# Sparse attention with a gated product behind it: scores over 232 keys instead of 256

## The chip, the cores and the metric

The kernel runs on one core of a Trainium2 chip. The metric is the device time of one execution in microseconds (us); the time of a version is the median over its runs. A core has the engines TensorE (PE; its weight loads are shown apart as PEld), VectorE (DVE), ScalarE (ACT), GpSimd (POOL) and SyncE (SP, which issues the DMA transfers here). Each works through its own queue of instructions in order.

## The reference

Inputs are q, k and v of 4 batches, 8 heads, 768 positions and 64 columns in float32, the numbers n_global = 8 and n_local = 96, and three weight matrices that reach the kernel as 64-bit floats. For each batch and head:

```
scores = q @ k.T / 8
rel = query position - key position
keep = (key < n_global) | ((rel >= 0) & (rel < n_local))
dist = n_local where only the first condition keeps the key, else |rel|
scores = scores - 2**-(head + 1) * dist, -1e9 where not kept
a = softmax(scores) (the sum gets 1e-9 added)
x = a @ v, put together as (3072, 512)
```

The result is `(x @ w_a * (x @ w_b)) @ w_out`, with w_a and w_b of 512 x 1536 and w_out of 1536 x 512. A query at position p needs the first 8 keys and the 96 keys that end with p. For a block of 128 queries that makes 8 first keys, up to 95 keys ahead of the block and its own 128.

## The kernel before

The 3072 positions are 24 blocks of 128 queries, six to a batch. They are put into eight units of 4, 2, 3, 3, 3, 3, 3 and 3 blocks. For each unit the attention is computed and then the product (here called the projection stage). The attention of unit u + 1 is computed during the projection stage of unit u, so that all engines share both kinds of work; only unit 0's attention stands alone at the start, beside the loading of the weights.

**Keys of a block (class Plan, L61 to L107).** Each block but the first of a batch is given a window of 256 keys: G = 32 first keys, the LW = 96 ahead and its own 128. Block 0 has its 128 own keys alone. Block 1's window of 256 is block 0's window and its own keys behind it (`joined`), so their keys are stored once. `kkeys` is the list of the unit's key columns, `kwin` the start and width of each block's window in it, `vkeys` and `vslot` the value chunks of 128 rows. The host packs q, k and v in this order (`pack`), and a DMA brings the keys and queries of a head (`fetch`, tile raw) or the values of two heads (`fetch_v`, tile v).

**Scores.** Units 2 to 7 (L784 to L801): `split` makes of the queries a rounded part qh and a rest ql, and of the keys a tile kk whose 128 partitions hold the rounded part and the rest (L351 is the subtraction, L341 and L343 are the copies); two float32r matmuls per block and head (L793) accumulate `ps[:, :w]`. Units 0 and 1 (`quad`, L668 to L679): full float32 matmuls (L673) straight from raw, for two blocks and the two heads of a pair, each with 64 partitions. A full float32 matmul leaves two records in the trace.

**Softmax (L530 to L600).** For each window: one VectorE operation adds the bias from the tile rel (`negd`; col or `negd0` for block 0) and finds the row's extreme (L537); ScalarE takes the exponential with its sum (L553); two small VectorE operations make the reciprocal (L568, L575); the normalisation is done by ScalarE (L585) or VectorE (L587). Each costs by the window's width w.

**Transposes and values.** `turn` (L602) transposes the window in chunks of 128 columns on TensorE (L609) and copies them out of PSUM; `values` (L614) multiplies each chunk with its value chunk (L626).

**Projection stage (L815 to L927).** For each of 12 columns blocks f of the weights: matmuls L851 with 128 times the unit's blocks columns (512, 256 or 384), their product on VectorE (L890), the split of it, and matmuls L869 of 512 columns. The weights are loaded and turned into a float32r part and a rest during unit 0's projection stage (`load_w`, L359 to L435), for each f in two halves of 768 columns: ScalarE L381 and L418, VectorE L388, L398, L408, L427, a copy L341 or L343 and a subtraction L351.

**Order.** `Schedule.order` (L193) is a list scheduler on the host. Every operation has a due time and estimated costs on the engines that may do it (functions act, dve, pool and pe), and the order and the choice of engine follow from these. The costs of scores, softmax and key splits are functions of w and hk.

**Start.** `build_positions` and `build_masks` make rel and col: VectorE and GpSimd operations over 256 and 128 columns, once.

Of the kernel before, what the change touches and what calls it, by code (L numbers as in the profile page):

```python
# [12 lines left out]
F32 = mybir.dt.float32  # L13
# [5 lines left out]
ALU = mybir.AluOpType  # L19
# [3 lines left out]
B, H, S, D = 4, 8, 768, 64  # L23
DM, DFF = 512, 1536
P = 128
# [2 lines left out]
NF = DFF // P  # L28
WN = 3 * 512 // 2
NT = B * S  # L30
G = 32
LW = 96

PAIRED = 2
# [14 lines left out]
BIG = float(2**38)  # L49
# [11 lines left out]
class Plan:  # L61
# [4 lines left out]
    def __init__(self, blocks, paired):  # L66
        self.nb = len(blocks)
        self.kkeys = []
        self.vkeys = []
        self.kwin = []  # L70
        self.vslot = []
        self.parts = []
        for n, (b, blk) in enumerate(blocks):
            if blk == 0:
                keys = np.arange(P)
            else:
                q0 = blk * P
                keys = np.concatenate([np.arange(G), np.arange(q0 - LW, q0 + P)])
            joined = blk == 1 and n > 0
            if paired and n % 2 == 0:  # L80
                self.parts.append(len(self.kkeys))
            if joined:
                self.kwin.append((self.kwin[-1][0], 2 * P))
                self.kkeys += [(b, j) for j in keys[P:]]
                self.vslot.append([self.vslot[-1][0], len(self.vkeys)])
                self.vkeys.append((b, keys[P:]))
            else:
                self.kwin.append((len(self.kkeys), len(keys)))
                self.kkeys += [(b, j) for j in keys]
                slots = []  # L90
                for c in range(len(keys) // P):
                    slots.append(len(self.vkeys))
                    self.vkeys.append((b, keys[c * P : (c + 1) * P]))
                self.vslot.append(slots)
        self.nk = len(self.kkeys)
        self.nv = len(self.vkeys)
        self.k0 = self.nb * P
        self.ncol = self.k0 + self.nk // 2
        if paired:

            ends = self.parts[1:] + [self.nk]
            self.pieces = []
            at = 0
            for k, end in zip(self.parts, ends):
                self.pieces.append((at, at + 2 * P - k, 2 * P + end - k, (k, end)))
                at += 2 * P + end - k
            self.ncol = at  # L107
# [198 lines left out]
class Fast:  # L306
# [223 lines left out]
    def softmax(self, h, due, wins, ps, t, sm):  # L530

        nc, op, n = self.nc, self.plan.op, len(wins)
        for j, (o, w) in enumerate(wins):
            neg = self.negd if w == 2 * P else self.negd0
            op(
                due,
                lambda e, j=j, o=o, w=w, neg=neg: nc.vector.tensor_tensor_reduce(  # L537
                    t[:, o : o + w],
                    ps[:, o : o + w],
                    neg[:, :w],  # L540
                    -(2.0 ** -(h + 1)),
                    3.0e38,
                    ALU.add,
                    ALU.min,
                    sm[:, j : j + 1],
                ),
                [ps, neg],
                [(t, j), (sm, j)],
                dve=dve(w) + 10,
            )  # L550
            op(
                due,
                lambda e, j=j, o=o, w=w: nc.scalar.activation(  # L553
                    t[:, o : o + w],
                    t[:, o : o + w],
                    AF.Exp,
                    bias=sm[:, j : j + 1],
                    scale=-1.0,
                    accum_out=sm[:, n + j : n + j + 1],
                ),  # L560
                [(sm, j)],
                [(t, j), (sm, n + j)],
                act=act(w) + 200,
            )
        sums = [(sm, n + j) for j in range(n)]
        op(
            due,
            lambda e: nc.vector.tensor_scalar_add(sm[:, 2 * n : 3 * n], sm[:, n : 2 * n], 1e-9),  # L568
            sums,
            [(sm, "e")],  # L570
            dve=69,
        )
        op(
            due,
            lambda e: nc.vector.reciprocal(sm[:, 3 * n : 4 * n], sm[:, 2 * n : 3 * n]),  # L575
            [(sm, "e")],
            [(sm, "r")],
            dve=75,
        )
        for j, (o, w) in enumerate(wins):  # L580

            def norm(e, j=j, o=o, w=w):
                r = sm[:, 3 * n + j : 3 * n + j + 1]
                if e == "act":
                    nc.scalar.mul(t[:, o : o + w], t[:, o : o + w], r)  # L585
                else:
                    self.engine(e).tensor_scalar(  # L587
                        t[:, o : o + w], t[:, o : o + w], r, 1.0, op0=ALU.mult, op1=ALU.mult
                    )

            op(
                due,
                norm,
                [(sm, "r")],
                [(t, j)],
                port=BOTH,
                dve=130 + 0.52 * w,
                pool=243 + 0.836 * w,
                act=act(w) + 100,
            )  # L600

    def turn(self, due, wins, t, pt, pf):  # L602

        nc = self.nc
        w = sum(w for o, w in wins)

        def emit(e):
            for c in range(0, w, P):
                nc.tensor.transpose(pt[:, c : c + P], t[:, c : c + P], self.ident)  # L609

        self.plan.op(due, emit, [t], [pt], pe=w / P * 109)
        self.copy(due, lambda: pf[:, :w], lambda: pt[:, :w], w, [pt], [pf], psum=True)

    def values(self, due, pl, blocks, v, probs, pa):  # L614

# [22 lines left out]
    def quad(self, u, c, j, due, raw, v, pa, homes):  # L638


        nc, pl, op, sp = self.nc, PLANS[u], self.plan.op, self.sbuf
        at, k0, _, _ = pl.pieces[j]
        blocks = (2 * j, 2 * j + 1)
        n = f"{u}_{c}_{j}"
        wins, o = [], 0
# [5 lines left out]
        qs, q0 = (raw, at) if scaled else (sp([P, cols], F32, tag, "qs" + n, 2), 0)  # L651
# [31 lines left out]
        for s in range(2):  # L683
            turn = 2 * (len(pl.pieces) * c + j) + s
            pick = lambda k: homes[k][turn % len(homes[k])]
            tag, cols = pick("t")
            t = sp([P, cols], F32, tag, f"t{s}_{n}", 2)
            sm = sp([P, 8], F32, "sm", f"sm{s}_{n}", 6)
            self.softmax(2 * c + s, due, wins, ps[s], t, sm)
            pt = self.bank(pick("pt"), f"pt{s}_{n}")  # L690
            pf = t
            if homes["pf"]:
                tag, cols = pick("pf")
                pf = sp([P, cols], F32, tag, f"pf{s}_{n}", 2)
            self.turn(due, wins, t, pt, pf)
            for i, (o, w) in zip(blocks, wins):
                probs[s, i] = (pf, o)
        if pa is None:
            pa = self.bank("psS", f"pa{n}")
        self.values(due, pl, blocks, v, probs, pa)  # L700
# [467 lines left out]
def build_positions(nc, cp, tp):  # L1168


    rel = cp.tile([P, 2 * P], F32, name="rel")
    col = cp.tile([P, P], F32, name="col")
    for t, step, base, mult in ((rel, -1, P, 1), (col, 1, 0, 0)):
        nc.gpsimd.iota(
            t,
            [[step, t.shape[1]]],
            base=base,
            channel_multiplier=mult,
            allow_small_or_imprecise_dtypes=True,
        )  # L1180
    t = tp.tile([P, 2 * P], F32, name="after")
    nc.vector.tensor_scalar(t, rel, 0.0, BIG, op0=ALU.is_lt, op1=ALU.mult)
    nc.vector.tensor_tensor(rel, rel, t, op=ALU.max)
    return rel, col, t


def build_masks(nc, rel, col, t, nf):

    v, ng, nl = nc.vector, nf[:, 0:1], nf[:, 1:2]
    v.tensor_scalar(t, rel, nl, -BIG, op0=ALU.is_ge, op1=ALU.mult)
    v.tensor_scalar(col, col, ng, -BIG, op0=ALU.is_ge, op1=ALU.mult)
    v.tensor_sub(rel, t, rel)
    v.tensor_scalar(col, col, nl, None, op0=ALU.subtract)
    v.tensor_copy(rel[:, :G], col[:, :G])
    v.tensor_tensor(col, rel[:, P:], col, op=ALU.max)


def build_scales(nc, cp):  # L1200
# [21 lines left out]
def build(nc, a, out):  # L1222
    with tile.TileContext(nc) as tc, ExitStack() as ctx:
        cp = ctx.enter_context(tc.tile_pool(name="c", bufs=1))
        with tc.manual_schedule(), tc.tile_pool(name="tmp", bufs=1) as tp:
# [2 lines left out]
            lim = build_limits(nc, cp)  # L1228
            spare = cp.tile([P, 1], F32, name="spare")
            nc.scalar.activation(spare, lim[:, 0:1], AF.Exp)  # L1230
            rel, col, t = build_positions(nc, cp, tp)
            sc = build_scales(nc, cp)
            raw0 = build_first(nc, cp, a["qkv"], sc)
            ident = cp.tile([P, P], F32, name="ident")
            make_identity(nc, ident)
            nf = build_counts(nc, cp, nv)
            flag = build_flag(nc, cp, nf, lim)
            build_masks(nc, rel, col, t, nf)
        fast = nc.values_load(flag[0:1, 0:1], min_val=0, max_val=2**30)
        inner = ctx.enter_context(ExitStack())  # L1240
        main = Fast(inner, tc, a["qkv"], a["wts"], out, raw0, (rel, col, sc, ident))
# [10 lines left out]
def pack(q, k, v):  # L1252
# [6 lines left out]
    for u, (blocks, pl) in enumerate(zip(UNITS, PLANS)):  # L1259
# [19 lines left out]
                        cols.append(np.vstack(a))  # L1279
                put(QOFFS[u][c], np.hstack(cols))  # L1280
        for c in range(NCC):
            vs = [v[b, 2 * c + s, keys] for s in range(2) for b, keys in pl.vkeys]
            put(VOFFS[u][c], np.hstack(vs))
    return flat

# [30 lines left out]
```

## Time and profile before

| what | value |
| --- | --- |
| time, median of 3 runs | 778.75 us (777.14 to 778.99) |
| profiled execution: time | 777.36 us |
| profiled execution: span of the trace | 775.1 us |
| TensorE, weight loads, VectorE, ScalarE, GpSimd busy | 751.5, 663.6, 438.7, 433.7, 6.6 us |
| mean granted TensorE clock | 0.995 of full |
| DMA | 58.04 MB, 75 GB/s in the mean |

The span is the time from the first to the last instruction on the core; 2.26 us of the profiled execution's time lie outside it. An engine's busy time is the union of its instructions' times. Matmuls overlap in their pipeline, so the duration of one is longer than the time for which it holds the queue.

### The profile page before, as it was taken

The numbers are of one execution on the slowest core, as the hardware profiler recorded it, in microseconds if no ns is written. First come the engines' busy times: TensorE is split into PE (matmuls) and PEld (weight loads), VectorE is DVE, ScalarE is ACT, GpSimd is POOL, SyncE is SP. The second block draws the span as 40 slices with busy tenths as digits, with TensorE's granted clock in tenths as the row PEclk, the third lists the DMA queues.
The fourth block names the chain that finished last, engine by engine and source line by source line (L and its number), as shares of the span: only waits on it lengthen the run. The fifth ranks groups of instructions, "written<-read, shape, count | busy, mean of one in ns | idle before, by whom it ended". The sixth has DMA issues, their size and how long they took to land.

```text
span 775.1 us, 12558 instructions
## 1 busy us (share of the span) xinstructions
PE 751.5 (97%) x4608; PEld 663.6 (86%) x4608; DVE 438.7 (57%) x1375; ACT 433.7 (56%) x1093; POOL 6.6 (1%) x24
## 2 busy tenths in 40 slices
PE   5799999999999999999999999999999999999997
PEld 4567777798998998989988988999988999889996
DVE  6999999766655654445554554455554545522111
ACT  6999756466656556455555565555544655442111
POOL 1000000000000000000000000000000000000000
PEclk9999999999999999999999999999999999999999
DMA  7888101032221111211112111111112121000001
GB/s 287 334 321 340 35 14 31 32 107 65 75 90 41 62 38 49 72 48 49 43 54 89 42 62 48 48 60 48 52 42 62 62 62 41 0 28 15 1 1 45
DMA packets 20086, 58.04 MB, mean 75 GB/s; under 512 B 2352, under 2 KB 2608, under 8 KB 20016
## 3 DMA queue, kind: packets, MB, share of 16 engines
q1 hardware_dynamic: 20016, 57.16, 21.5%
q8 instruction: 38, 0.62, 0.3%
q14 instruction: 32, 0.26, 0.1%
HBM read 50.86 MB, written 6.29 MB: 74 GB/s over the span
## 4 chain that ended last, share of the span: by engine, by line
PE 84%; DVE 7%; ACT 6%; issue 1%; DMA 1%; ACTq 0%; DVEq 0%
PE p L851 45%; PE acc L869 23%; PE pt L609 5%; PE pa L626 5%; PE ps L793 4%; PE ps L673 1%; ACT wr L418 1%; DVE kk L351 1%; DVE t L537 1%; ACT t L553 1%; ACT t L585 1%; ACT wm L381 1%; DVE wm L408 1%; ACT pf L341 1%; DVE wt L351 1%
## 5 line engine op out<-in xcount | busy, mean ns | idle before, releaser
L851 PE MATMUL p<-xh,wt 128*128 128x384 f32 (+2 forms) x1488 | 438.9, 345 | 4.0 <-DVE wt L343 2.3
L851 PEld LDWEIGHTS p<-xh,wt 128*128 128x128 f32 x1488 | 272.9, 189 | 18.2 <-issue 3.6
L851 PE MATMUL p<-xl,wt 128*128 128x384 f32 (+2 forms) x816 | 269.8, 342 | 0.2 <-DVE xl L351 0.2
L869 PE MATMUL acc<-wt,hh 128*128 128x512 f32 x576 | 206.4, 397 | 0.0
L851 PEld LDWEIGHTS p<-xl,wt 128*128 128x128 f32 x816 | 153.8, 189 | 10.3 <-DVE xl L351 1.4
L890 DVE TENSOR_TENSOR raw<-p,raw 128x384 f32<-128x384 f32 (+2 forms) x96 | 53.4, 557 | 153.5 <-PE p L851 146.8
L869 PEld LDWEIGHTS acc<-wt,hh 128*128 128x128 f32 x576 | 108.3, 188 | 19.0 <-issue 0.5
L553 ACT ACTIVATE t<-t,sm 128x256 f32<-128x256 f32 (+1 forms) x192 | 93.8, 491 | 40.0 <-DVE sm L537 39.0
L869 PE MATMUL acc<-wt,hl 128*128 128x512 f32 x288 | 113.0, 392 | 0.0
L585 ACT ACTIVATE t<-t,sm 128x256 f32<-128x256 f32 (+1 forms) x140 | 68.7, 494 | 71.1 <-DVE sm L575 66.2
L537 DVE CUSTOM_DVE_ANT_0 t<-ps,rel 128x256 f32<-128x256 f32 x160 | 66.6, 421 | 66.9 <-PE ps L793 64.4
L341 ACT COPY raw<-p 128x384 f32<-128x384 f32 (+2 forms) x95 | 45.3, 477 | 70.7 <-PE p L851 70.1
L609 PE MATMUL pt<-ident,t 128*128 128x128 f32 x352 | 68.6, 280 | 5.3 <-ACT t L585 2.5
L341 ACT COPY pf<-pt 128x256 f32<-128x256 f32 (+3 forms) x151 | 56.2, 375 | 22.6 <-PE pt L609 21.6
L351 DVE TENSOR_TENSOR hl<-raw,hh 128x384 fp32r<-128x384 f32 (+2 forms) x96 | 53.4, 556 | 23.7 <-ACT hh L341 23.1
L609 PEld LDWEIGHTS pt<-ident,t 128*128 128x128 f32 x352 | 43.2, 140 | 25.5 <-ACT t L585 10.1
L341 ACT CAST hh<-raw 128x384 fp32r<-128x384 f32 (+2 forms) x85 | 43.6, 513 | 35.9 <-DVE raw L890 34.9
L869 PEld LDWEIGHTS acc<-wt,hl 128*128 128x128 f32 x288 | 54.2, 188 | 6.6
L568 DVE TENSOR_SCALAR sm<-sm 128x1 f32<-128x1 f32 (+1 forms) x168 | 25.7, 153 | 43.5 <-ACT t L553 42.4
L351 DVE TENSOR_TENSOR kk<-raw,kk 64x384 fp32r<-64x384 f32 (+1 forms) x90 | 44.2, 491 | 2.8
L626 PE MATMUL pa<-pf,v 128*64 128x128 f32 x640 | 42.8, 278 | 2.4 <-ACT pf L341 1.9
L626 PEld LDWEIGHTS pa<-pf,v 128*64 128x64 f32 x640 | 34.7, 136 | 11.6 <-issue 5.0
(78 smaller groups left out, 604.7 us busy)
## 6 DMA issues: line engine op xcount, KB each, us to landing
wr<-wts SPq DMA_DIRECT2D x24, 768.0 KB, 12.5
raw<-qkv SPq DMA_DIRECT2D x29, 384.0 KB, 3.0
raw<-qkv SPq DMA_DIRECT2D x24, 320.0 KB, 2.9
v<-qkv SPq DMA_DIRECT2D x16, 384.0 KB, 3.1
out<-o SPq DMA_DIRECT2D x23, 256.0 KB, 2.1
v<-qkv SPq DMA_DIRECT2D x16, 256.0 KB, 2.7
raw<-qkv SPq DMA_DIRECT2D x3, 640.0 KB, 6.0
raw<-qkv SPq DMA_DIRECT2D x1, 256.0 KB, 3.5
```

The lines of the kernel that those rows point to most:

```text
L341: self.nc.scalar.copy(out(), src())
L351: lambda e: self.engine(e).tensor_sub(out(), a(), b()),
L537: lambda e, j=j, o=o, w=w, neg=neg: nc.vector.tensor_tensor_reduce(t[:, o : o + w], ps[:, o : o + w], neg[:, :w], -(2.0 ** -(h + 1)), 3.0e ...
L553: lambda e, j=j, o=o, w=w: nc.scalar.activation(t[:, o : o + w], t[:, o : o + w], AF.Exp, bias=sm[:, j : j + 1], scale=-1.0, accum_out=sm[ ...
L568: lambda e: nc.vector.tensor_scalar_add(sm[:, 2 * n : 3 * n], sm[:, n : 2 * n], 1e-9),
L585: nc.scalar.mul(t[:, o : o + w], t[:, o : o + w], r)
L609: nc.tensor.transpose(pt[:, c : c + P], t[:, c : c + P], self.ident)
L626: nc.tensor.matmul(pa[D * s : D * s + D, i * P : i * P + P], v[:, v0 : v0 + D], pf[:, o + c * P : o + c * P + P], start=c == 0, stop=c == ...
L793: nc.tensor.matmul(ps[:, :w], q[:, i * P : i * P + P], kk[:, k0 : k0 + w], start=m == 0, stop=m == 1,)
L851: nc.tensor.matmul(p[:, :T], wt(), b[:, b0 : b0 + T], start=c == 0 and n == 0, stop=c == NCC - 1 and n == 2,)
L869: nc.tensor.matmul(acc[i][:, :], hs[:, i * P : i * P + P], wt(), start=f == 0 and n == 0, stop=f == NF - 1 and n == 2,)
L890: lambda e, asb=asb, pb=pb: nc.vector.tensor_mul(asb[:, :T], pb[:, :T], asb[:, :T]),
```

## The change

Score windows are 232 keys wide: the block's own 128, the 96 ahead and 8 first keys, in this order. Block 1 keeps 256 columns (its own 128 and block 0's, with block 0's keys stored as 32 to 127 and then 0 to 31), and block 0 keeps 128. Since 232 is not a multiple of 128, the second transposed chunk is the last 128 columns of the window, so that 24 columns are transposed twice; the value chunk for it has 24 rows of zeros and then the 104 rows of keys ahead and first keys. The tiles rel and col follow the new order of keys.

```diff
-G = 32
+G = 8
@@ class Plan
+            at, slot, q0 = len(self.kkeys), len(self.vkeys), blk * P
+            head = np.concatenate([np.arange(P - LW, P), np.arange(P - LW)])
+            if blk == 0:
+                own = np.arange(P, 2 * P) if (b, 1) in blocks else np.arange(0)
+                self.kwin.append((at + len(own), P))
+                self.kkeys += [(b, j) for j in own] + [(b, j) for j in head]
+                self.vslot.append([slot])
+                self.vkeys.append((b, head))
+            elif blk == 1 and n:
+                start, _ = self.kwin[-1]
+                self.kwin.append((start - P, 2 * P))
+                self.vslot.append([slot, self.vslot[-1][0]])
+                self.vkeys.append((b, np.arange(P, 2 * P)))
             else:
+                keys = np.concatenate([np.arange(q0, q0 + P), np.arange(q0 - LW, q0), np.arange(G)])
+                self.kwin.append((at, len(keys)))
                 self.kkeys += [(b, j) for j in keys]
+                self.vslot.append([slot, slot + 1])
+                self.vkeys += [(b, keys[:P]), (b, keys[P:])]
@@ def softmax
-            neg = self.negd if w == 2 * P else self.negd0
+            neg = self.negd if w > P else self.negd0
@@ def turn
-        w = sum(w for o, w in wins)
+        starts = []
+        for o, w in wins:
+            starts += [o] if w == P else [o, o + w - P]
+        n = len(starts) * P
         def emit(e):
-            for c in range(0, w, P):
-                nc.tensor.transpose(pt[:, c : c + P], t[:, c : c + P], self.ident)
+            for c, o in enumerate(starts):
+                nc.tensor.transpose(pt[:, c * P : c * P + P], t[:, o : o + P], self.ident)
@@ def quad
-            for i, (o, w) in zip(blocks, wins):
+            o = 0
+            for i in blocks:
                 probs[s, i] = (pf, o)
+                o += len(pl.vslot[i]) * P
@@ def build_positions
-    for t, step, base, mult in ((rel, -1, P, 1), (col, 1, 0, 0)):
+    first = tp.tile([P, P - LW], F32, name="first")
+    for t, base, step, mult in (
+        (rel[:, :P], 0, -1, 1),
+        (rel[:, P:], LW, -1, 1),
+        (first, 0, 1, 0),
+    ):
...
-    nc.vector.tensor_scalar(t, rel, 0.0, BIG, op0=ALU.is_lt, op1=ALU.mult)
-    nc.vector.tensor_tensor(rel, rel, t, op=ALU.max)
+    nc.vector.tensor_scalar(t[:, :P], rel[:, :P], 0.0, BIG, op0=ALU.is_lt, op1=ALU.mult)
+    nc.vector.tensor_tensor(rel[:, :P], rel[:, :P], t[:, :P], op=ALU.max)
@@ def build_masks
-    v.tensor_scalar(t, rel, nl, -BIG, op0=ALU.is_ge, op1=ALU.mult)
-    v.tensor_scalar(col, col, ng, -BIG, op0=ALU.is_ge, op1=ALU.mult)
-    v.tensor_sub(rel, t, rel)
-    v.tensor_scalar(col, col, nl, None, op0=ALU.subtract)
-    v.tensor_copy(rel[:, :G], col[:, :G])
-    v.tensor_tensor(col, rel[:, P:], col, op=ALU.max)
+    n = P + LW
+    v.tensor_scalar(t, rel[:, :n], nl, -BIG, op0=ALU.is_ge, op1=ALU.mult)
+    v.tensor_scalar(first, first, ng, -BIG, op0=ALU.is_ge, op1=ALU.mult)
+    v.tensor_sub(rel[:, :n], t, rel[:, :n])
+    v.tensor_scalar(rel[:, n:], first, nl, None, op0=ALU.subtract)
+    v.tensor_copy(col[:, :LW], rel[:, P - LW : P])
+    v.tensor_tensor(col[:, LW:], rel[:, : P - LW], rel[:, n:], op=ALU.max)
@@ def pack
-            vs = [v[b, 2 * c + s, keys] for s in range(2) for b, keys in pl.vkeys]
+            vs = [
+                np.vstack([np.zeros((P - len(keys), D), q.dtype), v[b, 2 * c + s, keys]])
+                for s in range(2)
+                for b, keys in pl.vkeys
+            ]
```

## Rows read from the trace of the kernel before

**Rows 1.** The page: the span, the engines' shares, the chain by engine.

```profile
span 775.1 us, 12558 instructions
...
PE 751.5 (97%) x4608; PEld 663.6 (86%) x4608; DVE 438.7 (57%) x1375; ACT 433.7 (56%) x1093; POOL 6.6 (1%) x24
...
PE 84%; DVE 7%; ACT 6%; issue 1%; DMA 1%; ACTq 0%; DVEq 0%
```

**Rows 2.** Busy time by stretch: PE, PEld, DVE, ACT, POOL, clock, DMA share, GB/s.

```profile
0.00:20.00 20.00, 12.05 (x84) 8.64 (x85) 13.06 (x75) 12.73 (x41) 2.20 (x18) 0.91 0.77 290
20.00:40.00 20.00, 13.82 (x131) 9.54 (x127) 18.39 (x75) 20.00 (x60) 0.00 (x0) 0.99 0.85 338
...
60.00:80.00 20.00, 19.78 (x101) 15.58 (x100) 19.82 (x41) 20.00 (x37) 0.00 (x0) 1.00 0.72 294
...
200.00:300.00 100.00, 99.21 (x665) 89.89 (x665) 56.77 (x197) 58.06 (x159) 0.00 (x0) 1.00 0.19 59
```

**Rows 3.** Waits of TensorE, 160 to 690 us: total, times, longest.

```profile
PE pt L609 <- ACT t L585: 1.9, 7, 0.5
PE ps L793 <- DVE sm L568: 0.2, 1, 0.2
PE pt L609 <- DVE sm L568: 0.2, 1, 0.2
```

**Rows 4.** Timeline of TensorE, a pair of 256 columns: start, duration, instruction.

```profile
163.15 0.28 PE L793 MATMUL ps<-kk,qh 128*128 128x256 f32 x1
163.26 0.28 PE L793 MATMUL ps<-kk,ql 128*128 128x256 f32 x1
163.38 0.28 PE L851 MATMUL p<-xh,wt 128*128 128x256 f32 x1
```

**Rows 5.** The same view, a pair of 128 columns.

```profile
173.39 0.22 PE L793 MATMUL ps<-kk,qh 128*128 128x128 f32 x1
173.45 0.28 PE L793 MATMUL ps<-kk,ql 128*128 128x128 f32 x1
173.56 0.33 PE L851 MATMUL p<-xh,wt 128*128 128x256 f32 x1
```

**Rows 6.** Groups by shape, whole span: count, busy us, mean ns, idle before.

```profile
L793 PE MATMUL ps<-kk,qh 128*128 128x256 f32 x120 | 34.0, 283 | 0.2 <-DVE sm L568 0.2
```

**Rows 7.** The chain in order of time: start, duration, projections of 512 and 384 columns, a pair.

```profile
107.70 5.60 PE p L851 x24
...
169.56 0.24 PE ps L793 x2
...
705.20 4.16 PE p L851 x24
```

**Rows 8.** Softmax groups by shape, whole span; the last row 0 to 100 us.

```profile
L537 DVE CUSTOM_DVE_ANT_0 t<-ps,rel 128x256 f32<-128x256 f32 x160 | 66.6, 421 | 66.9 <-PE ps L793 64.4 <-PE pt L609 0.8 <-PE ps L673 0.4
L537 DVE CUSTOM_DVE_ANT_0 t<-ps,col 128x128 f32<-128x128 f32 x32 | 9.1, 283 | 7.2 <-PE ps L793 5.0 <-PE ps L673 2.2
L553 ACT ACTIVATE t<-t,sm 128x256 f32<-128x256 f32 x160 | 81.1, 509 | 35.2 <-DVE sm L537 34.7
L553 ACT ACTIVATE t<-t,sm 128x128 f32<-128x128 f32 x32 | 12.8, 401 | 4.8 <-DVE sm L537 4.3
...
L553 ACT ACTIVATE t<-t,sm 128x256 f32<-128x256 f32 x32 | 16.2, 513 | 1.4 <-DVE sm L537 1.4
```

**Rows 9.** The chain in order of time: one set of unit 1's scores.

```profile
116.06 1.06 PE ps L673 x8
```

**Rows 10.** The chain in the first 100 us: first scores, first projection.

```profile
5.94 3.24 PE ps L673 x16
...
39.87 4.01 PE p L851 x10
```

**Rows 11.** Groups by shape, whole span: two operations of the weight conversion.

```profile
L388 DVE TENSOR_SCALAR wm<-wm 128x768 f32<-128x768 f32 x24 | 12.9, 553 | 0.5 <-ACT wm L381 0.4
L408 DVE SCALAR_TENSOR_TENSOR wm<-wr,wm 128x768 int32<-128x768 int32 x24 | 22.5, 949 | 0.0
```

More of the change, by code (lines that the diff above doesn't have):

```diff
@@ L73, in __init__ @@
         for n, (b, blk) in enumerate(blocks):
[L74 to L79, printed above, removed]
             if paired and n % 2 == 0:
                 self.parts.append(len(self.kkeys))
[L82 to L86, printed above, removed]
-            else:
-                self.kwin.append((len(self.kkeys), len(keys)))
+            at, slot, q0 = len(self.kkeys), len(self.vkeys), blk * P
[11 more added lines that the diff above has]
+                self.vkeys.append((b, np.arange(P, 2 * P)))
+            else:
+                keys = np.concatenate([np.arange(q0, q0 + P), np.arange(q0 - LW, q0), np.arange(G)])
+                self.kwin.append((at, len(keys)))
                 self.kkeys += [(b, j) for j in keys]
[L90 to L94, printed above, removed]
+                self.vslot.append([slot, slot + 1])
+                self.vkeys += [(b, keys[:P]), (b, keys[P:])]
         self.nk = len(self.kkeys)
@@ L604, in turn @@
         nc = self.nc
-        w = sum(w for o, w in wins)
+        starts = []
+        for o, w in wins:
+            starts += [o] if w == P else [o, o + w - P]
+        n = len(starts) * P
         def emit(e):
-            for c in range(0, w, P):
-                nc.tensor.transpose(pt[:, c : c + P], t[:, c : c + P], self.ident)
-        self.plan.op(due, emit, [t], [pt], pe=w / P * 109)
-        self.copy(due, lambda: pf[:, :w], lambda: pt[:, :w], w, [pt], [pf], psum=True)
+            for c, o in enumerate(starts):
+                nc.tensor.transpose(pt[:, c * P : c * P + P], t[:, o : o + P], self.ident)
+        self.plan.op(due, emit, [t], [pt], pe=len(starts) * 109)
+        self.copy(due, lambda: pf[:, :n], lambda: pt[:, :n], n, [pt], [pf], psum=True)
     def values(self, due, pl, blocks, v, probs, pa):
@@ L1180, in build_positions, with build_masks @@
         )
-    t = tp.tile([P, 2 * P], F32, name="after")
-    nc.vector.tensor_scalar(t, rel, 0.0, BIG, op0=ALU.is_lt, op1=ALU.mult)
-    nc.vector.tensor_tensor(rel, rel, t, op=ALU.max)
-    return rel, col, t
-def build_masks(nc, rel, col, t, nf):
-    v, ng, nl = nc.vector, nf[:, 0:1], nf[:, 1:2]
-    v.tensor_scalar(t, rel, nl, -BIG, op0=ALU.is_ge, op1=ALU.mult)
-    v.tensor_scalar(col, col, ng, -BIG, op0=ALU.is_ge, op1=ALU.mult)
-    v.tensor_sub(rel, t, rel)
-    v.tensor_scalar(col, col, nl, None, op0=ALU.subtract)
-    v.tensor_copy(rel[:, :G], col[:, :G])
-    v.tensor_tensor(col, rel[:, P:], col, op=ALU.max)
+    t = tp.tile([P, P + LW], F32, name="after")
+    nc.vector.tensor_scalar(t[:, :P], rel[:, :P], 0.0, BIG, op0=ALU.is_lt, op1=ALU.mult)
+    nc.vector.tensor_tensor(rel[:, :P], rel[:, :P], t[:, :P], op=ALU.max)
+    return rel, col, first, t
+def build_masks(nc, rel, col, first, t, nf):
+    v, ng, nl = nc.vector, nf[:, 0:1], nf[:, 1:2]
+    n = P + LW
[5 more added lines that the diff above has]
+    v.tensor_tensor(col[:, LW:], rel[:, : P - LW], rel[:, n:], op=ALU.max)
 def build_scales(nc, cp):
@@ L1230, in build @@
             nc.scalar.activation(spare, lim[:, 0:1], AF.Exp)
-            rel, col, t = build_positions(nc, cp, tp)
+            rel, col, first, t = build_positions(nc, cp, tp)
             sc = build_scales(nc, cp)
@@ L1237, in build @@
             flag = build_flag(nc, cp, nf, lim)
-            build_masks(nc, rel, col, t, nf)
+            build_masks(nc, rel, col, first, t, nf)
         fast = nc.values_load(flag[0:1, 0:1], min_val=0, max_val=2**30)
```

## The prediction

> **What bounds the kernel now.** I read the page's shares first. TensorE holds 751.5 of the 775.1 us, and the chain that ended last runs over it for 84%, over VectorE for 7% and ScalarE for 6% [rows 1]. A busy TensorE is not yet a bound, since its matmuls overlap, so I went on to the stretches. There are two stages. In the first 100 us VectorE and ScalarE are nearly full (18.39 and 20.00 of 20 us between 20 and 40, 19.82 and 20.00 between 60 and 80) because the weights are turned into float32 halves there; TensorE has little to do before 40 us. Between 200 and 300 us TensorE has 99.21 of 100 us, and VectorE and ScalarE 56.77 and 58.06 [rows 2]. The waits of TensorE between 160 and 690 us are three entries, 2.3 us in all [rows 3]. So after the start an instruction is worth what it takes off TensorE's own queue, and nothing that VectorE, ScalarE or the DMA saves there counts.
>
> **What a matmul of the queue costs.** The recorded durations (283 ns for a 256-column score matmul [rows 6]) are pipelined ends and don't add up to the span. What counts is the distance between starts. The pair of 256 columns starts at 163.15 and 163.26, and what follows starts at 163.38: 0.23 us for two [rows 4]; in the chain another pair has 0.24 [rows 7], so I take 235 ns. The pair of 128 columns starts at 173.39 and 173.45 and is followed at 173.56: 0.17 us for two [rows 5]. In the chain 24 matmuls of 512 columns take 5.60 us, 233 ns each, and 24 of 384 columns take 4.16 us, 173 ns each [rows 7]. From 512 down to 384 columns that is 0.47 ns per column; from 512 to 256 (half of 235, 117 ns) it is 0.45, and from 256 to the 60 ns of the first narrow one 0.45. I take 0.445, where the starts are read to 0.01 us: 24 columns are 10.7 ns.
>
> **The change part by part.** *Scores from unit 2 on (L793).* Only blocks 2 to 5 of a batch have the 232-key window; block 1 keeps 256 and block 0 keeps 128. Units 2 to 7 cover three batches, so 3 x 4 blocks x 8 heads = 96 pairs shrink, out of the 120 pairs of 256 columns [rows 6]. 96 x 2 x 10.7 ns = **2.05 us**, in the stage where TensorE is full. The price of exactly 232 columns is in no row. From above, the saving can't pass the column price. From below: in the 128-column pair the second matmul holds the queue for 0.11 us though its 128 columns are worth 0.06 [rows 5], so something else, by its place the next weights' load, can set a floor of some 0.11 us. If each 232-column matmul stood on that floor of 110 to 112 ns instead of 106, a pair would take 220 to 224 ns of 235 and the sum would be 1.05 to 1.45 us. I take 2.05, because the first narrow matmul went at 60 ns and the floor showed only where two narrow ones stood behind each other; 1.05 stays for the range.
>
> The Trainium skill gives another slope: "TensorE: Matmul & The Clock Gate", section "Back-to-back issue gap", has a sustained spacing of about 81 ns at 128 columns and 131 ns at 512 in a stream of loads and matmuls. An estimate from that page is 0.13 ns per column, 3.1 ns per matmul, 0.6 us for the 192. This trace agrees at 128 (0.17 us for two [rows 5]) and not at 512 (233 ns [rows 7]), so the measured slope decides.
>
> *Scores of units 0 and 1 (L673).* These are full float32 with two records per matmul. Four matmuls (8 records) of 256 columns hold the queue 1.06 us [rows 9], the two heads side by side, so four slots of 265 ns in a row. Each slot streams its columns twice; 24 columns less are 2 x 10.7 = 21 ns, 85 ns per set. Unit 1 has four such sets in the stage where TensorE is nearly full: **0.34 us**. Unit 0 has four sets of narrowed blocks too, on a chain that is partly TensorE's [rows 10]: 0.34 us at most, nothing at least; I take 0.2.
>
> *Softmax.* The reduction (L537) goes from 421 to 283 ns between 256 and 128 columns, 1.08 ns per column; the exponential (L553) from 509 to 401, 0.84 [rows 8]. So 26 ns and 20 ns less per window, 20 for a ScalarE normalisation as well, priced like L553. From unit 2 on this is hidden: the engines are at half [rows 2]. Before 100 us they are the bound. 32 exponentials of 256 columns fall there [rows 8]; unit 0 has 24 of them (blocks 1 to 3, 8 heads), of which 16 are narrowed, and the other 8 are unit 1's, all narrowed. So ScalarE saves 24 x 20 = 0.5 us, and 0.5 more if all 24 normalisations fall to it; VectorE saves 24 x 26 = 0.6. The chain changes from one engine to the other, so they don't all add. Nothing at least, 1.0 at most; I take **0.4 us**.
>
> *Start.* The first score matmul comes at 5.94 us [rows 10], behind the masks. The mask operations are narrower (224 or 128 instead of 256 columns, 32 instead of 128), one more index fill is issued on GpSimd, well before. I put this at 0.1 us, zero to 0.2; the later mask copies lie under the first score matmuls (3.24 us).
>
> *What stays.* The number of score matmuls, transposes, value matmuls, accumulator reads and DMA issues is the same: two chunks of 128 columns are still transposed, the second starting 24 columns before the end of the first, with zeros in the values' rows there. The transpose copies out of PSUM keep their width. The key splits (L351 and others) get 348 or 244 columns for 384 or 256, and the loads up to 732 columns for 768; both are off the path from unit 2 on. If the cover were gone, the key splits would save time, not cost it. Columns now begin at multiples of 232 in the key tile and at 104 in the transposed tile; no row shows an access with such a start. Nothing excludes a cost: from below it is zero, the nearest rows (windows beginning at 0, 128, 256) show no difference between starts. I take zero.
>
> *Sum.* 2.05 + 0.34 + 0.2 + 0.4 + 0.1 = 3.1 us. The profiled execution took 777.36 us, 2.26 more than its span, and would take 774.3. It lies 1.4 under the median of the three runs, 778.75, so the median is forecast at 778.75 - 3.1 = **775.6 us**, 0.40% less.
>
> **The planner.** The order of all operations comes from a list scheduler fed with estimated costs, and these change. So the order will differ in places. In the full stage this costs little, as TensorE's waits of 2.3 us in 530 are all that order could take or give. In the first 100 us it matters more.
>
> **Rivals.** *The weight-load floor (chance 0.2).* Each narrowed pair saves only 11 to 15 ns. 1.05 to 1.45 replaces 2.05; time 776.2 to 776.6. For it speaks the 0.11 us in [rows 5], against it the 0.06 us just before. By the flatter slope of the skill page it would be 777.1, which I count in here.
>
> *The start gives it back (0.2).* VectorE is full until 100 us, and the changed order may put one more half of a weight block, or a softmax group, ahead of what TensorE waits for. A half costs VectorE five operations: two like L388 (553 ns) and three like L408 (949 ns), together 3.95 us [rows 11]. If part or all of one lands ahead of the first projection at 39.87 us [rows 10], the 3.1 us are lost: 777 to 779.6, no change. For it speaks that both engines are full; against it that there is less work for them than before.
>
> *Slower (0.1).* The same mechanism with two such halves, 7.9 us: 778.75 - 3.1 + 7.9 = 783.5. It decides from 5.5 us of delay on (3.1 gained plus 2.3). In the same tenth, with one or two in a hundred, is that float32r matmuls of under 256 columns take more passes: four would be about 400 ns for 106, 192 x 295 = 57 us, 832. The 60 ns of the 128-column matmul [rows 5] speak plainly against it.
>
> **How the numbers follow.** The forecast has 0.5. A difference under 0.3%, 2.3 us, is about what a measurement of this kernel can't tell from none. The forecast lies 0.8 us beyond that line; it counts mostly as faster (0.45 of its 0.5), the floor rival gives 0.1 to faster and 0.1 to same, the start rival nearly all to same, with a few in a hundred for a lucky order. So faster 0.57, same 0.33, slower 0.10. Low end: the start's terms at their full bounds (0.6 + 0.14 + 0.1 = 0.84 more) and runs 1.6 below their median as before: 773.2, set to 773.0. High end: the floor rival is inside; of the start rival all but its worst: 778.8.
>
> **What would show it.** In the profile after: L793 with 96 pairs of 128x232, their starts 106 ns apart (110 or more: the floor; 400: passes); TensorE's waits between 160 and 690 us still about 2 us; stages from 160 us on shorter by 2 us in sum; L537 near 395 and L553 near 489 ns; the first projection near 39.3 us instead of 39.87. The prediction fails if that projection comes later by over a microsecond, or if the spacing does not follow the columns.

## The result and the profile after

The changed kernel takes 782.49 us (median of 5 runs, 779.25 to 782.61) beside 778.75 before: a ratio of 1.0041, with a 95% interval of 1.0024 to 1.0059. The ratio is that of the mean times; by it the kernel is 3.2 us slower (the medians differ by 3.7) where 3.1 us less was forecast, and the time lies outside the range. Its profiled execution took 782.55 us, near the median; that of before, 777.36, was at the low end of its runs, so the two spans (780.7 and 775.1) differ by more than the kernels do.

The page of the changed kernel, for [rows 1]: span, shares, chain by engine. In this kernel L800 is the score matmul that was L793, L858 and L876 are the projections (L851, L869), L614 the transposes (L609), L678 the scores of units 0 and 1 (L673), L539, L555 and L587 the bias, exponential and ScalarE normalisation (L537, L553, L585).

```profile
span 780.7 us, 12544 instructions
...
PE 756.5 (97%) x4608; PEld 667.0 (85%) x4608; DVE 430.6 (55%) x1377; ACT 433.4 (56%) x1092; POOL 5.6 (1%) x24
...
PE 85%; DVE 8%; ACT 4%; issue 1%; DMA 0%; ACTq 0%; DVEq 0%
```

Less work on VectorE, as meant, and more time on TensorE. The busy times from 40 to 60 us, for [rows 2], and of four short stretches within (columns as there; the number behind the POOL count is the granted clock):

```profile
40.00:60.00 20.00, 17.41 (x78) 13.16 (x79) 19.55 (x34) 19.08 (x29) 0.00 (x0) 0.85 0.91 360
...
50.00:52.00 2.00, 1.41 (x5) 0.86 (x5) 1.83 (x4) 2.00 (x3) 0.00 (x0) 1.00 0.93 301
52.00:54.00 2.00, 1.15 (x3) 0.97 (x4) 2.00 (x4) 2.00 (x4) 0.00 (x0) 0.72 1.03 415
54.00:56.00 2.00, 2.00 (x7) 1.54 (x6) 1.98 (x4) 2.00 (x4) 0.00 (x0) 0.50 0.96 402
56.00:58.00 2.00, 2.00 (x9) 1.64 (x8) 1.96 (x3) 1.31 (x2) 0.00 (x0) 0.92 1.05 431
```

The stretch from 40 to 60 us in the kernel before:

```profile
40.00:60.00 20.00, 19.34 (x94) 14.84 (x95) 19.54 (x35) 19.85 (x30) 0.00 (x0) 0.93 0.84 323
```

Between 40 and 60 us TensorE of the changed kernel has 2.6 us of idle time where it had 0.7, and behind it 3.4 us at the lower clock, 1.2 GHz. (Both kernels also have the lower clock from 40 to 42 us.) The prices per operation that I forecast are there. Groups by shape, for [rows 6] and [rows 8]:

```profile
L555 ACT ACTIVATE t<-t,sm 128x232 f32<-128x232 f32 x128 | 62.3, 487 | 21.6 <-DVE sm L539 20.9
...
L539 DVE CUSTOM_DVE_ANT_0 t<-ps,rel 128x232 f32<-128x232 f32 x128 | 49.8, 397 | 69.7 <-PE ps L800 66.2 <-PE pt L614 1.8 <-PE ps L678 0.6
...
L800 PE MATMUL ps<-kk,qh 128*128 128x232 f32 x96 | 27.0, 282 | 0.0
```

And the timeline of TensorE at one pair of 232 columns, for [rows 4]:

```profile
299.88 0.27 PE L800 MATMUL ps<-kk,qh 128*128 128x232 f32 x1
299.99 0.27 PE L800 MATMUL ps<-kk,ql 128*128 128x232 f32 x1
300.10 0.35 PE L858 MATMUL p<-xh,wt 128*128 128x384 f32 x1
```

The pair holds the queue 0.22 us where 256 columns held it 0.23 to 0.24: the narrower float32r matmuls are a little cheaper, not dearer. The chain shows what went the other way, for [rows 9] and [rows 7]: a set of unit 1's scores, then one block of weights of the last unit, in which there is no attention at all.

```profile
119.02 0.98 PE ps L678 x8
...
709.54 4.21 PE p L858 x24
713.75 2.09 PE acc L876 x9
```

The set fell from 1.06 to 0.98 us. But 24 matmuls of 384 columns, which the change does not touch, went from 4.16 to 4.21 us, and the nine of 512 columns behind them from this in the kernel before:

```profile
709.36 2.06 PE acc L869 x9
```

### The profile page after: what moved, and what is told of

Same layout as the page of the kernel before. It is cut to its first block, busy times and chain, and to the rows that moved or that the text cites. A ratio compares the mean times of both kernels' runs of the same rounds, so it can differ in the third digit from the quotient of the medians.

```text
span 780.7 us, 12544 instructions
## 1 busy us (share of the span) xinstructions
PE 756.5 (97%) x4608; PEld 667.0 (85%) x4608; DVE 430.6 (55%) x1377; ACT 433.4 (56%) x1092; POOL 5.6 (1%) x24
## 4 chain that ended last, share of the span: by engine, by line
PE 85%; DVE 8%; ACT 4%; issue 1%; DMA 0%; ACTq 0%; DVEq 0%
PE p L858 47%; PE acc L876 23%; PE pt L614 5%; PE pa L631 5%; PE ps L800 4%; DVE kk L353 2%; ACT t L587 1%; PE ps L678 1%; DVE ql L507 1%; ACT t L555 1%; DVE t L539 1%; DVE kk L345 1%; ACT pf L343 1%; ACT wr L420 1%; DVE hl L353 1%
## 5 line engine op out<-in xcount | busy, mean ns | idle before, releaser
L858 PE MATMUL p<-xh,wt 128*128 128x384 f32 (+2 forms) x1488 | 438.9, 346 | 4.0 <-ACT wt L343 2.5
L858 PEld LDWEIGHTS p<-xh,wt 128*128 128x128 f32 x1488 | 274.2, 189 | 17.7 <-ACT wt L343 2.8
L858 PE MATMUL p<-xl,wt 128*128 128x384 f32 (+2 forms) x816 | 271.2, 343 | 1.4 <-ACT xl L343 0.8
L876 PE MATMUL acc<-wt,hh 128*128 128x512 f32 x576 | 206.0, 400 | 0.0
L858 PEld LDWEIGHTS p<-xl,wt 128*128 128x128 f32 x816 | 154.6, 190 | 11.2 <-ACT xl L343 1.1
L876 PEld LDWEIGHTS acc<-wt,hh 128*128 128x128 f32 x576 | 108.3, 188 | 20.8 <-issue 0.5
L555 ACT ACTIVATE t<-t,sm 128x232 f32<-128x232 f32 (+2 forms) x192 | 91.2, 476 | 40.9 <-DVE sm L539 38.8
L876 PE MATMUL acc<-wt,hl 128*128 128x512 f32 x288 | 113.5, 394 | 0.1
L539 DVE CUSTOM_DVE_ANT_0 t<-ps,rel 128x232 f32<-128x232 f32 (+1 forms) x160 | 63.3, 402 | 85.7 <-PE ps L800 82.2
L587 ACT ACTIVATE t<-t,sm 128x232 f32<-128x232 f32 (+2 forms) x125 | 59.5, 481 | 59.6 <-DVE sm L577 57.8
L614 PE MATMUL pt<-ident,t 128*128 128x128 f32 x352 | 68.6, 282 | 5.0 <-DVE sm L570 2.5
L614 PEld LDWEIGHTS pt<-ident,t 128*128 128x128 f32 x352 | 43.6, 141 | 24.4 <-ACT t L587 10.5
L876 PEld LDWEIGHTS acc<-wt,hl 128*128 128x128 f32 x288 | 54.3, 189 | 7.6 <-DVE hl L353 0.5
L353 DVE TENSOR_TENSOR kk<-raw,kk 64x348 fp32r<-64x348 f32 (+1 forms) x91 | 42.2, 464 | 2.8
```

Source lines behind the costliest of these rows:

```text
L353: lambda e: self.engine(e).tensor_sub(out(), a(), b()),
L555: lambda e, j=j, o=o, w=w: nc.scalar.activation(t[:, o : o + w], t[:, o : o + w], AF.Exp, bias=sm[:, j : j + 1], scale=-1.0, accum_out=sm[ ...
L614: nc.tensor.transpose(pt[:, c * P : c * P + P], t[:, o : o + P], self.ident)
L858: nc.tensor.matmul(p[:, :T], wt(), b[:, b0 : b0 + T], start=c == 0 and n == 0, stop=c == NCC - 1 and n == 2,)
L876: nc.tensor.matmul(acc[i][:, :], hs[:, i * P : i * P + P], wt(), start=f == 0 and n == 0, stop=f == NF - 1 and n == 2,)
```

## The experiments

All are timed beside runs of the kernel before on the same chip (its median 778.49 to 778.75). "Windows" means the 232-key windows, "order" the sequence of operations that the planner makes, "tiles" the widths of the key and load tiles (768 columns each before; 696 and 732 after), which decide the addresses of all tiles behind them.

| run | windows | order | tiles | median us | ratio (95%) |
| --- | --- | --- | --- | --- | --- |
| before | 256 | old | old | 778.75 | 1 |
| after | 232 | new | new | 782.49 | 1.0041 (1.0024 to 1.0059) |
| e1 | 232 | old | new | 775.85 | 0.9964 (0.9951 to 0.9977) |
| e2 | 256 | new | old | 785.46 | 1.0090 (1.0077 to 1.0103) |
| e3 | 232 | new | old | 778.22 | 0.9997 (0.9988 to 1.0007) |
| e4 | 232 | old | old | 773.74 | 0.9935 (0.9922 to 0.9948) |
| f1 | 256 | old | old + 64 bytes | 779.11 | 1.0005 (0.9996 to 1.0014) |
| f2 | 256 | old | old + 128 bytes | 778.20 | 0.9996 (0.9987 to 1.0005) |
| f3 | 232 | new | new + 64 bytes | 778.49 | 0.9997 (0.9988 to 1.0006) |
| f4 | softmax alone 232 | old | old | 776.07 | 0.9966 (0.9954 to 0.9978) |
| g1 | 256 | new for units 0, 1 | old | 780.62 | 1.0031 (1.0020 to 1.0041) |
| g2 | 256 | new for units 2 to 7 | old | 782.96 | 1.0056 (1.0040 to 1.0072) |
| g3 | 232 | costs of 248 keys | old | 772.62 | 0.9927 (0.9910 to 0.9943) |
| g4 | 232 | costs of 216 keys | old | 777.24 | 0.9984 (0.9975 to 0.9994) |

My theory was the order (A), its rivals the addresses (B) and the windows themselves (C).

**e1, the order of before.** The width w that the cost functions get is that of the kernel before, likewise for key splits and loads; the operations themselves are those of the change:

```diff
+def cw(i, w):
+    return 2 * P if w > P else w
-                dve=dve(w) + 10,
+                dve=dve(cw(blks[j], w)) + 10,
...
-        op(due, scores, [qh, ql, kk], [ps], pe=2 * pe(w))
+        op(due, scores, [qh, ql, kk], [ps], pe=2 * pe(cw(UNITS[u][i][1], w)))
```

> The changed kernel, all of its 232-key windows, but the planner is fed the costs of the kernel before, so that the operations stand in the order of before. Theory A (the changed order loses what the narrower windows win): no late start, so 0.996 of before, near 775.7 us, with the second block of weights' first matmul near 50.5 us and not 52.85. Theory B (tiles at other addresses slow the wide matmuls, in the last unit too): stays near 782, the last unit near 78.0 us instead of 77.0. Theory C (the narrower windows themselves cost): stays near 782 though the start is that of before.

Measured 775.85: C falls, and theory A's number is met to 0.2 us. That is luck in part, as e4 shows: A took the windows' gain to be the forecast 3.1 us and the addresses to cost nothing, while the windows gain 5.1 and the addresses take 2.3 of it back. The second block of weights starts at 50.75 us (timeline of e1):

```profile
50.75 0.50 PE L865 MATMUL p<-xh,wt 128*128 128x512 f32 x1 [0.69 <-ACT raw L348]
```

But B's sign is there too. The last unit still has slow matmuls (chain of e1):

```profile
701.86 4.21 PE p L865 x24
```

**e2, the order of after with the kernel before.** The same helper the other way round (232 for the windows that the change narrows).

> The kernel before, with its 256-key windows, but the planner is fed the costs of the changed kernel, so that the operations stand in the order of after. Theory A: slower by what the order costs, 3.7 + 3.1 = 6.8 us, near 785.5 us, 1.009 of before, with the late start (first matmul of the second block of weights near 52.9 us). Theory B and theory C: near 779, 1.000, apart from what the start loses (at most 3.5 us).

Measured 785.46, theory A again. The order costs by itself, with windows and tiles untouched. (A's 6.8 us held the 3.7 us by which the median of after lay higher, and part of that is the addresses', so the close hit is luck in part too.)

**e3, the tiles of before.**

```diff
-MAXK = max(p.nk for p in PLANS[1:])
+MAXK = 3 * 2 * P
-MAXC = max(max(p.ncol for p in PLANS[1:]), 2 * WIDE // 2)
+MAXC = 3 * 2 * P
```

> The changed kernel with the tiles of keys and of loads kept as wide as before (768 columns each), so that all tiles lie at the addresses of before. Theory A: no change from after, 782.5 us, 1.004. Theory B: the last unit's time back from 78.0 to 77.0 us and about 1% off all matmuls of 384 and 512 columns, 776 to 778 us, 0.998.

Measured 778.22: theory B, not A. The two are not rivals; both hold. The last unit is that of before (chain of e3):

```profile
705.50 4.16 PE p L858 x24
709.66 2.06 PE acc L876 x9
```

**e4, both.**

> Both: the order of before and the tiles of before, with the 232-key windows. Theory A: as with the order alone, near 775.7. Theory B: as with the tiles alone, or lower by the start's 3 us. Theory C: near 780 or more in spite of both.

Measured 773.74, 0.65% under before: what A and B give together. From before to after there is now a path of single steps: windows (before to e4) -0.65%, order (e4 to e3) +0.62%, tiles (e3 to after) +0.44%; in us of 778.7 that is -5.1, +4.8 and +3.4. That they add up to what was measured is so by construction and checks nothing. Other paths give other steps: in the order of before the tiles cost 0.29%, 2.3 us (e4 to e1); with the new tiles the order costs 0.77%, 6.0 us (e1 to after), with 256-key windows 0.90%, 7.0 us (e2). Each step has some 0.15 to 0.2% of noise to either side, so these differences are hardly clear of it: tiles 2 to 3 us, order 5 to 7.

Matmul by matmul the tiles' loss can be followed, as e3 and after have the same sequence of operations on every engine. The last block of the last unit in the chain of after; then in e3 the first set of unit 1's scores and that block:

```profile
766.41 4.22 PE p L858 x24
```

```profile
117.33 0.98 PE ps L678 x8
...
761.53 4.16 PE p L858 x24
```

The changed kernel is 1.69 us behind at those scores (119.02; its 3.4 us at the lower clock lie before that), 4.04 at the last unit (709.54 beside 705.50) and 4.88 at its last block. So 3.2 us are lost along the way, 0.8 of them in the last unit.

**f1 to f3, what it is about the addresses.** An unused tile ahead of the attention's tiles:

```diff
         self.sp = ctx.enter_context(tc.tile_pool(name="s", bufs=1))
+        self.sp.tile([P, 16], F32, tag="pad", name="pad")
```

> The kernel before, unchanged but for an unused tile of 64 bytes per partition ahead of the attention's tiles, which moves all of them up by 64 bytes. The operands of the projection (xh, xl, hh, hl) then start at multiples of 128 bytes, as the weight tiles do; in the kernel before they start 64 bytes off. Theory T (matmuls slow down where both operands have the same place modulo 128 bytes): last unit 78.0 us instead of 77.0, the whole 2 to 3 us slower, near 781, 1.003. Rival U (what slows is some other address, or the uneven widths of the key and load tiles): no change, 778.7.

> The same with an unused tile of 128 bytes: all tiles 128 bytes up, so that the projection's operands are again 64 bytes off a multiple of 128. Theory T: no change, 778.7, last unit 77.0. Rival V (any move away from the addresses of before costs): near 781, last unit 78.

> The changed kernel with the unused tile of 64 bytes. The key and load tiles stay at their uneven widths. Theory T: as with the tiles of before, near 778.2 us, 0.9995, last unit 77.0. Rival U: stays at 782.5.

f3 came out as theory T said: 64 bytes per partition take the change's 0.44% away again, with the narrow key and load tiles in place, so that rival U falls. But f1 shows no difference (1.0005) where T wanted 1.003, so T falls as well, and V with f2 (0.9996). The last unit in the chain of f3, of f1 and of f2 (of these two its second block):

```profile
705.06 4.16 PE p L859 x24
709.23 2.06 PE acc L877 x9
```

```profile
711.92 4.18 PE p L852 x24
716.11 2.08 PE acc L870 x9
```

```profile
712.64 4.16 PE p L852 x24
716.80 2.10 PE acc L870 x9
```

In the last unit f1 and f2 are slower than before (4.16 and 2.06 us) though their whole time is not. In f1 an early gain stands against it: the 24 matmuls of 512 columns that took 5.60 us in unit 0's stage [rows 7] take 5.44 there:

```profile
107.89 5.44 PE p L852 x24
```

That moving the tiles behind the key and load tiles changes the pace of matmuls that are otherwise the same, and the time, is shown by e3 and f3. Which rule it follows is open: f2's shift slows the 512-column matmuls of the last unit alone, and place is not all there is. g3, further on, has the projection's tiles at the places of before, and the same sequence of matmuls in this block, and yet:

```profile
705.84 4.19 PE p L865 x24
710.03 2.08 PE acc L883 x9
```

So differences as small as those of f1 and f2 can't be laid to the place alone.

**f4, the softmax alone.** The stored keys of a window are 256 again (24 more first keys behind the 232), the scores are taken over all, the softmax operations over 232:

```diff
-keys = np.concatenate([np.arange(q0, q0 + P), np.arange(q0 - LW, q0), np.arange(G)])
+keys = np.concatenate([np.arange(q0, q0 + P), np.arange(q0 - LW, q0), np.arange(P - LW)])
...
-            self.softmax(2 * c + s, due, wins, ps[s], t, sm, ...)
+            self.softmax(2 * c + s, due, narrow, ps[s], t, sm, ...)
```

> Order and tiles of the kernel before. The score matmuls, the key splits and the loads keep 256 columns (24 more first keys behind each window of 232), and only the softmax operations work on 232 of them; the transposes are those of the change. Theory S (most of the gain of the narrower windows comes from the shorter chain between a score and its transpose, for which TensorE's weight load waits): 3 to 4 us faster, near 775, 0.9955, and the weight loads of the transposes wait some 5 us for ScalarE instead of 8.8. Theory M (it comes from the score matmuls): at most the start's 0.8 us, near 778.

Measured 776.07, between the two (775 and 778): 0.34%, 2.6 us for the softmax and the masks, and the rest of e4's gain, 0.31% or 2.4 us, for scores, key splits and loads, each with about 1 us of noise to either side. The waits of the transposes' weight loads for ScalarE between 165 and 685 us (total, times, longest), before, in f4 and in e4:

```profile
PEld pt L609 <- ACT t L585: 8.8, 23, 0.8
```

```profile
PEld pt L625 <- ACT t L598: 7.2, 20, 0.7
```

```profile
PEld pt L620 <- ACT t L593: 5.3, 19, 0.7
```

S wanted some 5 us in f4, where 7.2 are left. The stage itself shows the gain too. In the chains of f4 and of e4:

```profile
116.05 1.06 PE ps L689 x8
...
703.65 4.16 PE p L871 x24
```

```profile
115.26 0.98 PE ps L684 x8
...
699.94 4.16 PE p L865 x24
```

From the first set of unit 1's scores to the last unit it is 589.14 us before (116.06 to 705.20 [rows 9, rows 7]), 587.60 in f4 and 584.68 in e4. So narrower softmax operations alone take 1.5 us off the stage in which they were thought to be hidden, about as much as the waits fell (1.6).

**g1 and g2, where the order loses.** Costs of 232 keys for units 0 and 1 alone, or for the others alone:

```diff
-    return 232 if i > 1 else w
+    return 232 if i[1] > 1 and i[0] < 2 else w
```

> The kernel before (256 keys, its own tiles), with the changed kernel's costs in the planner for units 0 and 1 alone: the first 720 of 3623 operations stand as in the changed kernel, the later ones nearly as before. If the order's 6.8 us are lost in parts, this holds the start's share: first matmul of the second block of weights near 53 us instead of 50.7, about 2.5 us slower in all, near 781.2. If all of it comes from the start: near 785.5. If none: 778.7.

> The opposite: the costs of the changed kernel for units 2 to 7 alone; the first 733 operations stand as before. If the loss is in parts: the start as before, then 4 us lost in units 2 to 6, near 782.8, with the weight loads of the transposes waiting some 13 us for ScalarE between 165 and 685 us instead of 8.8. If all is the start's: 778.7.

Both parts are there: 2.1 and 4.5 us (each against 778.49), together 6.6 beside e2's 7.0. The timeline of g1, TensorE before the second block of weights, idle times in brackets:

```profile
50.02 0.49 PE L858 MATMUL p<-xl,wt 128*128 128x512 f32 x1 [0.68 <-ACT xl L346]
51.20 1.43 PE L858 MATMUL p<-xl,wt 128*128 128x512 f32 x5 [0.69 <-DVE xl L737]
53.60 0.50 PE L858 MATMUL p<-xh,wt 128*128 128x512 f32 x1 [0.97 <-ACT raw L346]
```

And the waits of the weight loads in g2, in the view of f4:

```profile
PEld pt L615 <- ACT t L591: 13.4, 31, 0.6
```

**g3 and g4, two more orders.** The helper with 248 and with 216.

> The changed kernel with its 232-key windows and the tiles of before, the planner fed as if windows were 248 wide: a third order. With the costs of 256 keys these windows took 773.74, with those of 232 keys 778.22. Theory P (the lower the costs, the closer the planner puts a transpose behind its softmax, and the more TensorE waits): between these, near 775. Theory L (a lottery: any change of the costs gives another order, good or bad without a trend): anywhere from 773 to 780.

> The same with the costs of 216 keys: a fourth order. Theory P: slower than with the costs of 232, near 781. Theory L: anywhere from 773 to 782, no trend.

772.62 and 777.24. With 256, 248, 232 and 216 keys in the costs the same operations take 773.74, 772.62, 778.22 and 777.24 us. That is no clean trend (P wanted 248 in between and 216 to be the slowest), rather two good orders and two bad ones. P falls; L, which excludes little, is left, and four orders can't settle more. g3 has the lowest median here, 0.73% under before, but its interval and e4's overlap.

## Why the prediction was wrong

The windows themselves gave more than forecast, 5.1 us (e4). What failed are two things that I put at little or nothing: the planner's order, which takes 4.8 us, and the addresses of the tiles, which take 3.4.

**The planner.** This step failed first. I wrote that in the full stage the order "costs little, as TensorE's waits of 2.3 us in 530 are all that order could take or give". g2 shows 4.5 us lost there, and e4 to e3 4.8 us for the order in all, start included. The view was the wrong one: a matmul's wait counts as idle only after the modelled end of the one before it, so that a wait of its weight load need not show in it. In the changed kernel that view has less than before, for [rows 3]:

```profile
PE pt L614 <- DVE sm L570: 0.3, 1, 0.3
```

The weight loads' own waits, 8.8 us before and 13.4 in g2, were the ones to read: they rise by 4.6 us where the time rises by 4.5 (in f4 they fall by 1.6 where the stage shortens by 1.5). In g2 the transposes stand so that the normalised softmax is not ready when TensorE comes to them. In the changed kernel the narrower windows shorten these waits and the order lengthens them, so that it stands near the kernel before. After, and e1, which has the order of before and all else as in after:

```profile
PEld pt L614 <- ACT t L587: 9.2, 28, 0.5
```

```profile
PEld pt L620 <- ACT t L593: 4.8, 17, 0.6
```

**The start.** The rival was named and priced, with a chance of 0.2, at the wrong place: I looked for a weight half ahead of the first projection, which came at 40.13 us beside 39.87 [rows 10]. The loss lies behind it. The timeline of TensorE in the changed kernel, then before:

```profile
49.24 0.50 PE L858 MATMUL p<-xl,wt 128*128 128x512 f32 x1 [0.76 <-ACT xl L343]
50.43 1.41 PE L858 MATMUL p<-xl,wt 128*128 128x512 f32 x5 [0.69 <-DVE xl L737]
52.85 0.78 PE L858 MATMUL p<-xh,wt 128*128 128x512 f32 x1 [1.01 <-ACT raw L343]
```

```profile
50.69 0.50 PE L851 MATMUL p<-xh,wt 128*128 128x512 f32 x1 [0.66 <-ACT raw L341]
```

ScalarE over the same time, after and then before:

```profile
47.03 0.88 ACT L343 CAST wt<-wm 128x768 fp32r<-128x768 f32 x1
47.75 0.97 ACT L420 ACTIVATE wr<-wr 128x768 int32<-128x768 uint32 x1
48.56 0.62 ACT L343 CAST xl<-pa 128x512 fp32r<-128x512 f32 x1
...
52.13 0.66 ACT L343 COPY raw<-p 128x512 f32<-128x512 f32 x1
```

```profile
47.23 0.59 ACT L341 CAST xl<-pa 128x512 fp32r<-128x512 f32 x1 [0.15 <-PE pa L626]
...
50.08 0.56 ACT L341 COPY raw<-p 128x512 f32<-128x512 f32 x1
```

The copy of unit 0's last attention output (xl) has two weight operations ahead of it and comes at 48.56 instead of 47.23 us. The copy out of the first projection's sum (raw) has four more after that, where it had three, and comes at 52.13 instead of 50.08 us. In the profiled execution 3.4 us at the lower clock followed, so that matmuls from 53.43 us on stand 0.42 us apart instead of 0.23. The profiles of e2, e3, f3 and g1, with the same order up to there, have the full clock from 52 to 58 us, so the order alone does not bring it; whether the other runs of the changed kernel had it was not recorded.

**What stays: addresses.** "I take zero" was written for the new column starts inside the key and transposed tiles; e4 has these starts and gains more than forecast, so nothing speaks for a cost there. What I didn't ask is where the other tiles go. Two key tiles of 288 bytes per partition less and two load tiles of 128 less (rounded) move everything behind them by 832 bytes, the projection's operands too: 3.4 us (2.3 in the order of before), on matmuls that the change doesn't touch. The sum had no term for it.

**The sum of the windows.** 3.1 us were forecast, 5.1 measured (e4). Softmax and start: 0.5 forecast, 2.6 measured (f4), because I costed the softmax from unit 2 on at nothing; f4's 1.5 us in the stage are that part. Some 20 ns less in each of three operations between a score and its transpose bring the transposes forward, and TensorE's weight loads wait less. The price per operation was right: 397 and 487 ns beside 395 and 489 forecast. Scores, key splits and loads: 2.05 + 0.34 + 0.2 = 2.6 forecast, 2.4 measured (e4 less f4). That agreement is luck in part. The pair of 232 columns takes 0.22 us of 0.235, nearer the floor rival's price than the column price (0.21): by these rows the scores' term was 96 x 0.015 = 1.4 us and not 2.05. And between f4 and e4 the weight loads' waits fell too, by 1.9 us, which no term of the forecast held.

An estimate from the slope in the Trainium skill ("TensorE: Matmul & The Clock Gate", section "Back-to-back issue gap") is 6 ns less for a pair. The trace has about 15, at 0.01 us a step.

The masks gave 0.18 us (first scores at 5.76 instead of 5.94 us), 0.1 forecast.

## What to carry to other kernels

When a change alters the numbers that a planner is fed, run it once with the old numbers: otherwise one measures another schedule too, and a good edit (here 0.65%) can be read as a loss. A tile whose size changes moves its neighbours, so hold the addresses when timing an edit, and try a small pad when untouched instructions change pace. On a full TensorE read the waits of its weight loads too: here the matmuls' idle time (2.3 us) understated what the order could cost, and work on other engines was not free where a transpose stood waiting behind it. Don't take a number that comes out as expected for a proof of its terms: e1's did, with two of them wrong.

## What the runs showed of the hardware

The distance between the starts of matmuls changed when tiles moved, by as little as 64 bytes per partition: with the same sequence of operations, the second block of the last unit took 4.22 us (24 matmuls of 384 columns) and 2.10 (nine of 512) in after, 4.16 and 2.06 in f3, and the times were 782.49 and 778.49 us. In the built programs the tile xh starts, modulo 512 bytes, at 64 (before), 128 (f1), 192 (f2), 256 (after) and 320 (f3), with the weight tiles in place; that block took 4.16, 4.18, 4.16, 4.22 and 4.16 us and 2.06, 2.08, 2.10, 2.10 and 2.06. The order of these operands in memory is the same in all five up to the exchange of hh and hl. A move can also speed up: in f1 24 matmuls of 512 columns took 5.44 us in unit 0's stage instead of 5.60. Why some places are slower was not found, and g3 has 4.19 and 2.08 at the places of before, so that something else, in its order or in that one execution, plays a part.
